# A recurrent attention with a token and channel mixer on one Trainium2 core: one batch's sum made transposed in PSUM, channel weights cut otherwise, and a new written-out order

## The chip, the core and the metric

The kernel runs on one core of one Trainium2 chip. The metric is the device time of one execution in microseconds, as the median of several runs. The profile is one execution that the hardware profiler recorded; its times count from the start of the program's span.

## What is computed

A gated linear recurrence over 768 tokens, for 4 batches and 8 heads of 48, is followed by a mixer over tokens and then over channels:

```python
for t in range(S):                                   # S = 768, D = 48, B = 4, H = 8
    state = alpha[:, :, t, :, None] * state + einsum('bhd,bhe->bhde', k[:, :, t], v[:, :, t])
    y[:, :, t] = einsum('bhd,bhde->bhe', q[:, :, t], state)
x  = y as (B, S, H * D)                              # (4, 768, 384)
h  = relu(x^T @ w_tok1) @ w_tok2                     # 768 -> 256 -> 768, over tokens
u  = x + h^T
h2 = relu(u @ w_ch1) @ w_ch2                         # 384 -> 1536 -> 384, over channels
out = u + h2
```

## The kernel before, in words

Each batch has three attention chunks of 256 tokens, numbered 0 to 11 over the four batches (chunk n belongs to batch n // 3). A chunk loads alpha, k, q and v (`ld_at`, `ld_kt`, `ld_qt`, `ld_vt`, 384 KB each), makes the decays, the masked scores and the state, and leaves two tiles `x` of 128 tokens by 384 channels. The mixer of a batch then runs, in the names of the plan:

- `t1_b_m_kc`: w_tok1 against the six x tiles, 12 matmuls of 384 columns; `ht_b_m` is the relu into bf16.
- `t2_b_i` (L883): w_tok2 against the two `ht` tiles, two matmuls for each of six token blocks; `u_b_i` (L887) is VectorE's addition of x, into the tile `u`.
- The transpose of u into `ut`. Batch 0 (`UP = (0,)`) does it on TensorE: `up_0_p` (L894), six 128 by 128 transposes for each pair of blocks, and `ut_0_p` (L746, L745), a copy of 768 columns out of PSUM. Batches 1 to 3 do it with two DMA transposes, `ux_b_half` (L729), issued from SyncE.
- `c1_b_mc_half` (L902): 12 chunks of hidden channels by two halves of the tokens, three matmuls each; `rt_b_mc_half` is the relu, on ScalarE (L873) or VectorE (L875).
- `c2_b_i_q` (L907): four groups of three matmuls for each block; `o_b_i` (L911) adds u, `st_b_i` stores 192 KB.

The weights come as fp32 loads (`ldw_`) that are cast to bf16 (`cw_`, L745 and L746): w_tok1 in two pieces, w_tok2 in two, w_ch1 in six and w_ch2 in six, 384 KB each. A piece of w_ch1 before the change is 128 rows by 768 hidden channels, so a `c1` of the chunks 0 to 5 needs the pieces 0, 1, 2 and one of the chunks 6 to 11 the pieces 3, 4, 5; in the order, chunk 11 comes first, behind the pieces 4, 3 and 5.

No scheduler runs on the device. The string `ORDER` names every operation in turn with its engine (t TensorE, s ScalarE, v VectorE, g GpSimd, y SyncE's DMA queue), and `BUFS` the buffer of every value. Each engine and each DMA queue works its own operations in that order and waits for what an operation needs. All loads and DMA transposes go through SyncE's queue, the stores through SyncE's or ScalarE's. The 19 buffers `in` hold what was loaded until it was used. Operations named `f1_` to `f12_` are fillers: matmuls over a tile of zeros (`fill`) that write a bank that nobody reads.

```python
for o in order:
    g.port_turn = o.on if o.port and o.on in ("DVE", "POOL") else None
    o.emit(o.on)
```

Of the kernel before, what the change touches and what calls it, by code (L numbers as in the profile page):

```python
# [9 lines left out]
BF16 = mybir.dt.bfloat16  # L10
# [91 lines left out]
UP = (0,)  # L102
# [18 lines left out]
def build(g):  # L121
# [8 lines left out]
    def fillers():  # L130
        for o in list(P.ops):
            nm = o.name
            if "PE" in o.eng and (nm[:4] in ("t1_0", "t2_0", "up_0") or nm.split("_")[-1][-1] in "0123" and nm[:2] not in ("t1", "t2", "up", "c1", "c2") and not nm.endswith("10") and not nm.endswith("11")):
# [182 lines left out]
    def mixer(b):  # L316
# [15 lines left out]
        us = []  # L332
        for i in range(NS):
            if i % 3 == 0:
                u = V("u")
            bank = V("one")
            o = P.op(f"t2_{b}_{i}", pe([384] * 2), m0 + (1900 + 330 * i) * sc, writes=[bank],
                     reads=[h for h, _ in hts], preds=[h for _, h in hts] + [wl[("wt2", p)] for p in range(2)],
                     emit=lambda e, i=i, bank=bank: g.tok2(bank, i, [h for h, _ in hts]))
            uo = P.op(f"u_{b}_{i}", dve(384), m0 + (1950 + 330 * i) * sc, writes=[u], reads=[bank, x[i][0]], preds=[o],  # L340
                      emit=lambda e, i=i, bank=bank, u=u: g.uadd(u, i, bank, x[i][0]))
            us.append((u, uo))
        ut = V("ut")
        uts = []
        if b in UP:
            for p in range(3):
                bank = V("one")
                o = P.op(f"up_{b}_{p}", pe([128] * 6), m0 + (3900 + 340 * p) * sc, writes=[bank],
                         reads=list(dict.fromkeys([us[2 * p][0], us[2 * p + 1][0]])),
                         preds=[us[2 * p][1], us[2 * p + 1][1]],  # L350
                         emit=lambda e, p=p, bank=bank: g.utr(bank, [us[2 * p][0], us[2 * p + 1][0]], p))
                uts.append(P.op(f"ut_{b}_{p}", either(dve(768, True), act(768)), m0 + (3950 + 340 * p) * sc, writes=[ut],
                                reads=[bank], preds=[o], emit=lambda e, p=p, bank=bank: g.utev(e, ut, bank, p)))
        else:
# [18 lines left out]
        for i in range(NS):  # L373
            hold = 4000.0 if (i >= NS - 3 and b < B - 1) else 0.0
            cuts = [(0, HD // 2), (HD // 2, HD)] if (b, i) == LAST else [(0, HD)]
            for ci, (ca, cz) in enumerate(cuts):
# [3 lines left out]
                for q4 in range(4):  # L380
                    pp = []
                    for mc in range(3 * q4, 3 * q4 + 3):
# [6 lines left out]
                          reads=[bank, us[i][0]], preds=[prev],  # L389
# [25 lines left out]
trq2t ld_at3y vs1_2g ldw_wt11y evq2v ib1t y1_1t y0_1t vs0_2g ldw_wt21y sm1_1g P3g K2t sa0_2v sm0_2g x0_1s t1_0_0_0t
f1_G0_2t G0_2t ldw_wt20y G1_2t cw_wt20g t1_0_1_0t mask0_2v x1_1s t1_0_1_1t ld_at4y ld_kt3y t1_0_1_2t lnP3s cum3t
cw_wt11s IE3s ia2t y0_2t x0_2s t1_0_0_1t t1_0_0_2t E3s t1_0_0_3t mask1_2v t1_0_1_3t ib2t y1_2t ldw_wc14y t1_0_1_4t
x1_2s t1_0_0_4t f1_t1_0_1_5t t1_0_1_5t ht_0_1v P4g cw_wt21s t1_0_0_5t ht_0_0s f3_t2_0_0t t2_0_0t t2_0_1t u_0_0v ln13s
r13s ldw_wc13y t2_0_2t u_0_1v t2_0_3t u_0_2v t2_0_5t lnP4s t2_0_4t u_0_3v u_0_5v u_0_4v up_0_0t cw_wc14s cw_wc13s
ldw_wc15y up_0_1t ld_qt3y k0a3g kk3g cum4t trk3t cw_wc15g ut_0_0v up_0_2t ut_0_2v ut_0_1s c1_0_11_0t c1_0_8_0t IE4s  # L420
c1_0_11_1t rt_0_8_0v rt_0_11_0v ldw_wc11y q0r3g qq3g c1_0_9_1t rt_0_9_1v ln14s kb3s c1_0_10_0t cw_wc11s c1_0_9_0t
rt_0_9_0v rt_0_11_1v E4s c1_0_7_0t c1_0_10_1t c1_0_7_1t ldw_wc10y r14s cw_wc10s rt_0_10_1v trq3t evk3s rt_0_7_0v
ldw_wc12y ld_vt3y cw_wc12g c1_0_2_0t c1_0_0_1t ka3g rt_0_7_1s c1_0_8_1t rt_0_10_0v vb3v vs1_3g vs0_3g rt_0_0_1v
rt_0_2_0v evq3s ld_at5y ld_qt4y c1_0_1_1t rt_0_8_1v c1_0_3_0t kc3s K3t P5g c1_0_4_1t rt_0_3_0s rt_0_1_1s q0r4g G0_3t
ld_kt4y qq4g s0_3v ln15s G1_3t sa1_3v c1_0_2_1t rt_0_2_1s mask0_3v lnP5s c1_0_1_0t c1_0_5_1t rt_0_5_1s rt_0_1_0s r15s
mask1_3v ldw_wc21y cw_wc21s k0a4g ldw_wc20y c1_0_6_1t rt_0_6_1v c1_0_4_0t kk4v ldw_wc22y c1_0_5_0t c1_0_0_0t cw_wc22s
rt_0_4_0v rt_0_0_0v cw_wc20g rt_0_4_1s c1_0_6_0t rt_0_6_0v c1_0_3_1t trq4t rt_0_3_1v cum5t trk4t ld_kt5y k0a5g
ldw_wc23y rt_0_5_0s c2_0_3_0t c2_0_5_0t evq4s kb4s evk4v ld_qt5y G1_4t mask1_4v G0_4t ld_vt4y c2_0_0_0t IE5s c2_0_0_1t
ka4g cw_wc23s c2_0_3_1t kc4s sm1_3g E5s mask0_4v ib3t y1_3t ldw_wc24y cw_wc24s c2_0_5_1t vb4g vs1_4s x1_3s ia4t
ldw_wc25y vs0_4g cw_wc25s ld_at6y y0_3t kk5v c2_0_3_2t y0_4t q0r5v trk5t evk5s qq5v K4t c2_0_0_2t sa0_4v c2_0_0_3t P6v  # L430
x0_3s ld_at7y sm0_4g o_0_0v trq5t x0_4s sa1_4v P7g evq5s lnP6s c2_0_5_2t c2_0_5_3t ld_vt5y vb5g c2_0_4_0t c2_0_4_1t
ld_kt7y kc5g G1_5t G0_5t lnP7s o_0_5v ib4t y1_4t vs1_5s mask1_5v t1_1_1_0t t1_1_1_1t sm1_4g x1_4s c2_0_4_2t c2_0_3_3t
# [61 lines left out]
class Emit:  # L494
# [386 lines left out]
    def tok2(self, bank, i, hts):  # L881
        for kc in range(NDT):
            self.pe.matmul(self.bank(bank)[:, 0:HD], lhsT=self.wt2[:, kc, i * 128 : i * 128 + 128], rhs=self.t(hts[kc]),  # L883
                           start=(kc == 0), stop=(kc == NDT - 1))
# [81 lines left out]
```

## Time and profile before

| what | value |
|---|---|
| device time, 3 runs | 162.30, 162.38, 162.38 us; median 162.38 |
| span of the profiled execution | 160.5 us |
| time of the runs outside such a span | 162.38 - 160.5 = 1.9 us |
| instructions | 3971 |
| TensorE busy | 154.6 us (96%), 1563 matmuls |
| VectorE, ScalarE, GpSimd busy | 114.9, 97.8, 80.8 us (72%, 61%, 50%) |
| DMA | 35.05 MB in 76130 packets, mean 218 GB/s |

The page gives the busy time of each engine, the span in 40 slices (a digit is the busy share in tenths), the DMA queues, and groups of instructions by line. The span leaves out what lies before the program's first and behind its last instruction; the profiled execution itself has no time of its own beside its span, so the median of the runs stands for it. In a timeline row stand the start, the time, engine, line, what is written and read, and the count.

### The profile page before, as it was taken

To read this page: it belongs to the slowest core of one execution; us is meant where nothing else is said; L and a number is where in the kernel's file an instruction comes from. 1 tells how busy PE (TensorE), PEld (TensorE's weight loads), DVE (VectorE), ACT (ScalarE), POOL (GpSimd) and SP (SyncE) were. 2 spreads that over 40 slices of the span, in tenths; PEclk is the share of its full clock that TensorE was granted. 3 is DMA by queue.
4 is the path that set the end of the run, shared out by engine and by line. 5 is a ranking of instruction groups with operands and counts; after the bars stand their busy time and mean duration, and the time that the engine had idled before them with its cause. 6 is when DMAs were issued, how large, how long until landed. Compare 5 with 4: busy or idle time off the path is not lost.

```text
span 160.5 us, 3971 instructions
## 1 busy us (share of the span) xinstructions
PE 154.6 (96%) x1563; PEld 97.1 (60%) x1563; DVE 114.9 (72%) x206; ACT 97.8 (61%) x179; POOL 80.8 (50%) x94
## 2 busy tenths in 40 slices
PE   7999989999999999999999999999999999999992
PEld 2545565766667676666667666566567665665661
DVE  6099994979889787989969758795886762464222
ACT  3789999998899955897563583269832203343000
POOL 5205897695973649389778852699523000000000
PEclk9999999999999999999999999999999999999999
DMA  4999999999999999999989999989701235111133
GB/s 122 320 324 317 317 374 311 339 333 306 316 347 324 275 278 272 210 228 319 241 202 298 239 315 204 217 196 134 196 21 62 87 79 169 49 49 53 49 129 116
DMA packets 76130, 35.05 MB, mean 218 GB/s; under 512 B 70352, under 2 KB 74320, under 8 KB 76112
## 3 DMA queue, kind: packets, MB, share of 16 engines
q1 hardware_dynamic: 73808, 31.76, 74.1%
q10 hardware_dynamic: 2304, 3.05, 5.3%
q8 instruction: 12, 0.20, 0.5%
q14 instruction: 6, 0.05, 0.1%
HBM read 25.17 MB, written 4.72 MB: 186 GB/s over the span
## 4 chain that ended last, share of the span: by engine, by line
PE 61%; DMA 12%; DVE 6%; ACT 6%; SPq 6%; POOL 4%; issue 3%; DVEq 0%; POOLq 0%
PE ps L907 22%; PE ps L902 21%; PE ps L643 11%; DMA in<-in_v_dram 6%; SPq L584 6%; DMA out_dram<-o 4%; PE ps L878 3%; PE ps L883 2%; DMA ut<-u 2%; DVE pkk L700 2%; DVE gtm L770 1%; PE ps L712 1%; DVE rt L875 1%; POOL vb L746 1%; POOL pkq L700 1%
## 5 line engine op out<-in xcount | busy, mean ns | idle before, releaser
L907 PE MATMUL ps<-wc,rt 128*128 128x384 bf16 (+1 forms) x300 | 52.4, 319 | 0.0
L902 PE MATMUL ps<-ut,wc 128*128 128x384 bf16 x288 | 50.3, 326 | 0.1
L902 PEld LDWEIGHTS <-wc 128*128 128x128 bf16 x288 | 27.1, 98 | 17.9 <-DMA ut<-u 0.6
L907 PEld LDWEIGHTS <-rt 128*128 128x128 bf16 x300 | 27.8, 98 | 16.0
L873 ACT ACTIVATE rt<-ps 128x384 bf16<-128x384 f32 x47 | 21.4, 492 | 23.6 <-PE ps L902 23.3
L875 DVE TENSOR_SCALAR rt<-ps 128x384 bf16<-128x384 f32 x49 | 25.6, 551 | 9.1 <-PE ps L902 8.9
L770 DVE TENSOR_TENSOR gtm<-ps,mk 128x1024 bf16<-128x1024 f32 x24 | 28.5, 1218 | 3.1 <-PE ps L643 2.8
L911 DVE TENSOR_TENSOR o<-ps,u 128x384 f32<-128x384 f32 (+1 forms) x25 | 13.2, 536 | 12.6 <-PE ps L907 10.1
L700 POOL TENSOR_TENSOR pkk<-in,IE 128x768 bf16<-128x768 f32 x8 | 14.5, 1817 | 3.3 <-DVE ss L844 2.3
L745 ACT CAST x<-ps 128x384 bf16<-128x384 f32 x20 | 9.2, 479 | 11.1 <-PE ps L643 9.5
L887 DVE TENSOR_TENSOR u<-ps,x 128x384 bf16<-128x384 f32 x24 | 12.0, 550 | 3.1 <-PE ps L883 2.5
L746 POOL CAST vb<-in 64x384 bf16<-64x384 f32 (+1 forms) x14 | 8.3, 594 | 10.4 <-DMA in<-in_v_dram 4.7
L692 POOL TENSOR_TENSOR in<-in,in 128x384 f32<-128x384 f32 x8 | 8.0, 1000 | 10.5 <-DVE u L887 3.8
L643 PE MATMUL ps<-rt 128*128 128x512 bf16 (+1 forms) x29 | 12.1, 515 | 1.1 <-DVE rt L541 1.1
L745 ACT CAST vb<-in 64x384 bf16<-64x384 f32 (+1 forms) x18 | 11.4, 634 | 0.8 <-DMA in<-in_v_dram 0.3
L700 POOL TENSOR_TENSOR pkq<-in,E 128x768 bf16<-128x768 f32 x6 | 10.9, 1818 | 0.6 <-DMA tpk<-pkq 0.3
L878 PE MATMUL ps<-x,wt 128*128 128x384 bf16 x48 | 11.0, 325 | 0.0
L844 POOL TENSOR_TENSOR ss<-tmp,E 128x384 bf16<-128x384 f32 x10 | 8.3, 833 | 4.2 <-DVE in L628 3.9
L841 DVE TENSOR_TENSOR tmp<-ps,ss 128x384 f32<-128x384 f32 x16 | 8.8, 552 | 1.8 <-PE ps L643 0.6
L883 PE MATMUL ps<-ht,wt 128*128 128x384 bf16 x48 | 9.1, 326 | 0.0
L643 PE MATMUL ps<-vb,gtm 128*128 128x48 bf16 x192 | 8.2, 183 | 0.2 <-DVE gtm L770 0.2
L643 PE MATMUL ps<-tpq,tpk 48*64 48x128 bf16 (+1 forms) x288 | 7.9, 218 | 0.4 <-POOL tpq L746 0.3
(94 smaller groups left out, 207.6 us busy)
## 6 DMA issues: line engine op xcount, KB each, us to landing
in<-in_alpha_dram SPq DMA_DIRECT2D x12, 384.0 KB, 5.1
in<-in_v_dram SPq DMA_DIRECT2D x12, 384.0 KB, 5.6
in<-in_k_dram SPq DMA_DIRECT2D x12, 384.0 KB, 5.2
in<-in_q_dram SPq DMA_DIRECT2D x12, 384.0 KB, 5.5
in<-in_moe_w_ch_dram SPq DMA_DIRECT2D x12, 384.0 KB, 5.9
out_dram<-o ACTq DMA_DIRECT2D x15, 192.0 KB, 1.8
in<-in_moe_w_tok_dram SPq DMA_DIRECT2D x4, 384.0 KB, 6.0
out_dram<-o SPq DMA_DIRECT2D x8, 192.0 KB, 2.2
```

The source lines that it names most:

```text
L643: return self.pe.matmul(out, lhsT=lhsT, rhs=rhs, start=start, stop=stop, skip_group_check=True)
L700: self.shared(self.eng[e].tensor_tensor(self.t(dst)[:, :, h0:h1, 0:D], self.t(src)[:, h0:h1].rearrange("p h s d -> p s h d"), bass.AP(tens ...
L745: return self.act.copy(d, s)
L770: self.nc.vector.tensor_tensor(self.t(gtm)[:, hf, :, :], self.pair(gp).rearrange("p a (j t) -> p (a j) t", t=128), bass.AP(tensor=m.tensor ...
L873: self.act.activation(d, s, AF.Relu)
L875: self.nc.vector.tensor_scalar_max(d, s, 0.0)
L878: self.pe.matmul(self.bank(bank)[:, 0:HD], lhsT=self.wt1[:, kc, m * 128 : m * 128 + 128], rhs=self.t(x), start=(kc == 0), stop=(kc == NS - 1))
L883: self.pe.matmul(self.bank(bank)[:, 0:HD], lhsT=self.wt2[:, kc, i * 128 : i * 128 + 128], rhs=self.t(hts[kc]), start=(kc == 0), stop=(kc = ...
L887: self.nc.vector.tensor_tensor(self.t(u)[:, i % 3], self.bank(bank)[:, 0:HD], self.t(x), ALU.add)
L902: self.pe.matmul(self.bank(bank)[:, 0:HD], lhsT=self.wc1[:, kc, mc * 128 : mc * 128 + 128], rhs=self.t(ut)[:, 3 * half : 3 * half + 3, kc, ...
L907: self.pe.matmul(self.bank(bank)[:, 0 : cz - ca], lhsT=self.t(rts[mc][0])[:, i * 128 : i * 128 + 128], rhs=self.wc2[:, mc, ca:cz], start=( ...
L911: self.nc.vector.tensor_tensor(self.t(o)[:, ca:cz], self.bank(bank)[:, 0 : cz - ca], self.t(u)[:, i % 3, ca:cz], ALU.add)
```

## The change

For batch 0 (`UDIR = (0,)`, `UP = ()`) u is made transposed at once. Each of six PSUM banks first gets three 128 by 128 matmuls of an x tile against the identity (`xa_0_half_j`), and then the product of the two `ht` tiles with a half of w_tok2 is added in the same bank (`tt_0_half_j`, two matmuls of 384 columns, operands swapped against `t2`). `ut_0_half_j` copies the bank (384 columns of fp32) to `ut`, on ScalarE or VectorE. VectorE's six additions `u_0_i` and the PSUM transposes are gone. The output still needs u with tokens in the partitions: two DMA transposes `un_0_half` from `ut` to `u`, on SyncE's queue, and `o_0_i` waits for them.

The w_ch1 pieces become three row blocks by 256 hidden channels, so `c1_b_mc` waits for the one piece `mc // 2`; their runs in memory are 1 KB long in place of 3 KB. The w_tok2 pieces become halves of the tokens, so a `t2` or `tt` waits for one piece. `ORDER` and `BUFS` are new from end to end. Tokens are in natural order in both kernels.

In the new order, SyncE's queue starts `ld_at0 ld_vt0 ld_kt0 ld_at2 ld_at1 ld_qt0`; the first `c1` of batch 0 waits for the 20th load (`ldw_wc14`) where it waited for the 22nd. Fillers are fewer: `f8_cumw0 f1_cumw0 f6_trk0 f1_trk0 f2_G0_1 f2_trk2 f1_trq2 f2_t1_0_1_0` stand in place of thirteen.

```diff
-UP = (0,)
+UP = ()
+UDIR = (0,)
...
+        if b in UDIR:
+            ut, us, uts = V("ut"), [], []
+            for half in range(2):
+                evs = []
+                for j in range(NM):
+                    bank = V("one")
+                    tx = x[3 * half : 3 * half + 3]
+                    xa = P.op(f"xa_{b}_{half}_{j}", pe([128] * 3), m0 + (1700 + 900 * half + 60 * j) * sc, writes=[bank],
...
+                    o = P.op(f"tt_{b}_{half}_{j}", pe([384] * 2), m0 + (1900 + 900 * half + 330 * j) * sc, writes=[bank],
+                             reads=[h for h, _ in hts], preds=[h for _, h in hts] + [xa, wl[("wt2", half)]],
...
+                    evs.append(P.op(f"ut_{b}_{half}_{j}", either(act(384), dve(384)), m0 + (1950 + 900 * half + 330 * j) * sc,
...
+                un = P.op(f"un_{b}_{half}", {"SP": (1240.0, 1240.0)}, m0 + 6000 * sc, writes=[u], reads=[ut], preds=evs,
+                          emit=lambda e, u=u, half=half: g.unat(u, ut, half), dma=("x", 1450.0, 1180.0, 480.0))
...
-                         reads=[ut], preds=(uts[0:2 + half] if b in UP else [uts[half]]) + [wl[("wc1", p)] for p in ((0, 1, 2) if mc < 6 else (3, 4, 5))],
+                         reads=[ut], preds=(uts[half] if b in UDIR else uts[0:2 + half] if b in UP else [uts[half]]) + [wl[("wc1", mc // 2)]],
...
-                          reads=[bank, us[i][0]], preds=[prev],
+                          reads=[bank, us[i][0]], preds=[prev, us[i][1]],
...
         elif nm == "wc1":
-            c, h = piece % 3, piece // 3
-            self.gated(dma(t, self.w[2][128 * c : 128 * c + 128, 768 * h : 768 * h + 768]), op)
+            w = self.w[2].rearrange("(c p) m -> p c m", p=128)
+            self.gated(dma(t.rearrange("p (c m) -> p c m", c=3), w[:, :, 256 * piece : 256 * piece + 256]), op)
...
+    def xadd(self, bank, xs, j):
+        for i, x in enumerate(xs):
+            self.mm(self.bank(bank)[:, i * 128 : i * 128 + 128], self.t(x)[:, j * 128 : j * 128 + 128], self.idn, i == 0, False)
+
+    def tok2t(self, bank, half, j, hts):
+        for kc in range(NDT):
+            self.mm(self.bank(bank)[:, 0:HD], self.t(hts[kc])[:, j * 128 : j * 128 + 128],
+                    self.wt2[:, half, kc, :], False, kc == NDT - 1)
...
+    def unat(self, u, ut, half):
+        self.nc.sync.dma_start_transpose(self.t(u).rearrange("p i (j c) -> p (i j) c", j=NM),
+                                         self.t(ut)[:, 3 * half : 3 * half + 3].rearrange("p i j t -> p (i j t)"))
```

The parts of the new order that the prediction speaks of (SyncE's queue up to the first transpose of batch 1, and TensorE around the first `c1` of batch 0 and of batch 1):

```
SyncE before: ... ldw_wc24 ldw_wc25 ld_at6 ld_at7 ld_vt5 ld_kt7 ld_at8 ld_kt6 ld_qt6 ld_qt7 ld_kt8 ld_vt6 dk6 ux_1_0
SyncE after:  ... ld_qt5 ldw_wc25 un_0_1 ld_vt5 un_0_0 ld_at6 ld_at7 ld_at8 ld_vt6 ld_qt6 ld_kt6 ld_kt7 ld_qt7 ux_1_0 ld_vt7 dk6 ux_1_1
PE after:     ... t1_0_0_5 xa_0_1_2 trq3 xa_0_1_1 tt_0_0_0 tt_0_0_2 tt_0_0_1 tt_0_1_0 tt_0_1_2 tt_0_1_1 c1_0_9_0 c1_0_8_0 trk3 c1_0_0_0
PE after:     ... t2_1_0 t2_1_5 c2_0_5_0 c2_0_5_1 c2_0_5_2 t2_1_3 t2_1_4 cum7 c2_0_5_3 c2_0_0_3 cum8 c1_1_8_0
ACT after:    ... x1_2 IE3 ht_0_1 ht_0_0 cw_wt21 ut_0_0_0 cw_wc14 ut_0_1_1
```

More of the change, by code (lines that the diff above doesn't have):

```diff
@@ L132, in fillers @@
             nm = o.name
-            if "PE" in o.eng and (nm[:4] in ("t1_0", "t2_0", "up_0") or nm.split("_")[-1][-1] in "0123" and nm[:2] not in ("t1", "t2", "up", "c1", "c2") and not nm.endswith("10") and not nm.endswith("11")):
+            if "PE" in o.eng and (nm[:4] in ("t1_0", "t2_0", "up_0", "xa_0", "tt_0") or nm.split("_")[-1][-1] in "0123" and nm[:2] not in ("t1", "t2", "up", "c1", "c2", "xa", "tt") and not nm.endswith("10") and not nm.endswith("11")):
                 bank = V("one")
@@ L331, in mixer @@
             hts.append((ht, ho))
-        us = []
-        for i in range(NS):
-            if i % 3 == 0:
-                u = V("u")
[L336 to L342, printed above, removed]
@@ L415 @@
[L415 to L419, printed above, removed]
@@ L420 @@
[L420 to L424, printed above, removed]
```

188 lines of the change are left out of this document (110 added, 78 removed), and 22 rows, old and new, of the table BUFS.

## The prediction

> **What bounds the kernel now.** I read the page first, then TensorE's waits, the windows, and the order of TensorE and of SyncE's queue around batch 0's and batch 1's first `c1`.
>
> ```profile
> span 160.5 us, 3971 instructions
> ...
> PE   7999989999999999999999999999999999999992
> ...
> DMA  4999999999999999999989999989701235111133
> ```
>
> TensorE's digits are full from the second slice to the last but one. Its waits say the same of its input:
>
> ```profile
> PE ps L643 <- DVE rt L541: 1.1, 1, 1.1
> PE ps L643 <- ACT E L683: 0.4, 1, 0.4
> PE ps L643 <- DVE gtm L770: 0.3, 2, 0.2
> PE ps L643 <- POOL tpq L746: 0.3, 1, 0.3
> ```
>
> They total 2.1 us, and none is in a mixer. But the DMA digits are full too, up to the 20th slice (80 us). The windows tell how full:
>
> ```profile
> 0.00:20.00 20.00, 18.19 (x175) 9.39 (x176) 13.99 (x39) 15.24 (x20) 8.87 (x20) 1.00 1.01 280
> 20.00:40.00 20.00, 19.50 (x206) 12.34 (x206) 16.32 (x28) 18.68 (x34) 15.62 (x18) 1.00 1.06 333
> 40.00:55.00 15.00, 14.90 (x173) 10.22 (x173) 13.14 (x19) 14.06 (x25) 9.51 (x12) 1.00 1.03 317
> 55.00:65.00 10.00, 10.00 (x116) 6.60 (x114) 7.83 (x14) 5.79 (x14) 7.37 (x8) 1.00 1.03 269
> ```
>
> The columns after the stretch are TensorE, its weight loads, VectorE, ScalarE, GpSimd (busy us), then granted clock, DMA share and GB/s. The clock is 1.00 throughout, and the DMA share is over 1.00 in each stretch to 65 us. So two resources run side by side without a hole: TensorE's order, and the transfers of SyncE's queue. A change that helps one gains only as far as the other lets it. The place where they meet is batch 1's first `c1`, behind its first DMA transpose `ux_1_0`.
>
> **TensorE's side: batch 0 starts earlier.** These are TensorE's rows of batch 0 (the second is a filler):
>
> ```profile
> 25.58 0.37 PE L643 MATMUL ps<-vb,gtm 128*128 128x48 bf16 x8
> ...
> 26.94 0.86 PE L643 MATMUL ps<-rt 128*64 128x384 f32 x2
> 27.73 2.28 PE L883 MATMUL ps<-ht,wt 128*128 128x384 bf16 x12
> 29.85 0.83 PE L894 MATMUL ps<-idn,u 128*128 128x128 bf16 x12
> ...
> 30.81 0.61 PE L712 MATMUL ps<-idn,pkk 128*128 128x128 bf16 x8
> 31.25 0.50 PE L894 MATMUL ps<-idn,u 128*128 128x128 bf16 x6
> 31.76 2.44 PE L902 MATMUL ps<-ut,wc 128*128 128x384 bf16 x14
> ```
>
> The last attention product is at 25.58, `c1` starts at 31.76. The change moves the 18 identity products (0.83 + 0.50 us of rows) ahead of the relu, where fillers stood, and drops VectorE's additions and a copy from the chain. What is late next is ScalarE, by its own queue:
>
> ```profile
> 25.99 0.48 ACT L745 CAST x<-ps 128x384 bf16<-128x384 f32 x1
> 26.37 0.83 ACT L745 CAST wt<-in 128x768 bf16<-128x768 f32 x1
> 27.10 0.49 ACT L873 ACTIVATE ht<-ps 128x384 bf16<-128x384 f32 x1
> ...
> 28.88 1.67 ACT L745 CAST wc<-in 128x768 bf16<-128x768 f32 x2
> ```
>
> In the new queue, behind the last x cast (end 25.99 + 0.48 = 26.5, which I keep: its loads, v and q of chunk 2, are the 14th and 11th where they were the 12th and 11th), come: the last `t1` (0.3), two relus (0.5 each), the cast of a w_tok2 piece (0.8), the copy `ut_0_0_0` (0.5, as a relu of the same tile), and the cast of the w_ch1 piece (1.67 / 2 = 0.8) for which `c1_0_9_0` waits. Together 26.5 + 0.3 + 1.0 + 0.8 + 0.5 + 0.8 = 29.9, with handovers some 30.2. The six `tt` banks (2.28 us from about 28.0) end at about the same time. So `c1` starts 31.76 - 30.2 = 1.5 us earlier. `trk3` and `cum4`, which stood ahead of it, now stand behind, some 0.6 us by their rows' pitch less 0.3 for `trq3`, which came forward: a lead of 1.2 us is left. Fewer fillers are worth nothing by themselves; they sat in time that TensorE waited anyway. From here to `c1_1_8_0` both orders hold the same TensorE work (151 and 148 operations, apart from the renamed ones the same set), so TensorE alone would bring batch 1's first `c1` from 67.80 to 66.6.
>
> **The queue's side: what stands ahead of `ux_1_0`.**
>
> ```profile
> 57.47 1.77 SPq L584 DMA_DIRECT2D in<-in_k_dram  x1
> 59.29 1.61 SPq L584 DMA_DIRECT2D in<-in_v_dram  x1
> 62.89 1.33 SPq L725 DMA_TRANSPOSE tpk<-pkk  x1
> 64.68 1.29 SPq L729 DMA_TRANSPOSE ut<-u  x1
> ```
>
> ```profile
> DMA  9999999999999999974269969605999979739999
> GB/s 340 331 340 325 328 331 309 377 304 306 292 277 290 301 312 317 301 218 118 60 166 297 143 117 287 127 7 133 288 294 287 198 224 382 201 84 283 293 290 359
> ...
> in<-in_k_dram SPq DMA_DIRECT2D x1, 384.0 KB, 6.5
> in<-in_v_dram SPq DMA_DIRECT2D x1, 384.0 KB, 5.8
> ...
> out_dram<-o ACTq DMA_DIRECT2D x1, 192.0 KB, 2.0
> ut<-u SPq DMA_TRANSPOSE x2, 3.0
> tpk<-pkk SPq DMA_TRANSPOSE x1, 3.4
> ```
>
> ```profile
> 62.64 1.46 PE L883 MATMUL ps<-ht,wt 128*128 128x384 bf16 x8
> ...
> 67.80 1.46 PE L902 MATMUL ps<-ut,wc 128*128 128x384 bf16 x8
> ```
>
> The first fence is SyncE's issues, the second the DMA view of 59.2 to 69.0 (40 slices of 0.245 us; then KB and us to landing), the third TensorE there. The 48th load (`ld_kt8`) lands at 57.47 + 6.5 = 64.0, the 49th at 65.1, `dk6` at 66.3, `ux_1_0` at 64.68 + 3.0 = 67.7: in order of issue. `c1_1_8_0` follows at 67.80, so TensorE's order and the queue met within 0.1 to 0.2 us. The digits show the DMA idle for parts of 63.6 to 66.3, when `dk6` and `ux_1_0` waited for their data: so the true bound of the queue before was the 48th load's landing at 64.0, and it is this that I carry over.
>
> In the changed order 48 loads, of the same kinds and sizes (16 weights, 32 of attention), stand ahead of `ux_1_0`, one fewer, and `dk6` has moved behind. Ahead of it have come both `un_0` transposes, and on ScalarE's queue three stores, with a fourth just in front, where one was. Their prices: a transpose of u is 128 x 1152 bf16, 295 KB; the GB/s row has 288, 294 and 287 in the slices in which `ux_1_0` alone ran, so 295 / 290 = 1.0 us (0.9 at the 333 GB/s of the loads; 1.4 by the distance from `dk6`'s landing to `ux_1_0`'s, which holds some waiting, so I take the value of the rate). Two make 2.0 (1.8 to 2.8). A store is 197 KB, 0.6 us at 333 GB/s; two to three more make 1.5 (1.2 to 1.8). Next, the shorter runs of w_ch1:
>
> ```profile
> in<-in_moe_w_ch_dram SPq DMA_DIRECT2D x12, 384.0 KB, 5.9
> ...
> in<-in_moe_w_tok_dram SPq DMA_DIRECT2D x4, 384.0 KB, 6.0
> ```
>
> Half of the w_tok loads already have 1 KB runs, and the four land 0.1 us later than the w_ch loads with 3 KB ones. For eight loads that bounds it at 0 to 0.8; I take 0.1, since at full queue what counts is the rate and the windows with both kinds have 280 to 333 GB/s.
>
> So the 48th load lands at 64.0 + 2.0 + 1.5 + 0.1 = 67.6, and `ux_1_0`, queued behind it, at 68.6 (67.9 to 70.8 with all ends). It can't be issued past them: all of it is one queue, worked in order. `c1_1_8_0` starts at 68.65 in place of 67.80, though TensorE could have been there at 66.6. The lead of 1.2 us is lost in a new wait of 2.0 us, and 0.85 more with it. All that TensorE has left stands behind that `c1`.
>
> [...]
>
> **After that** the remaining TensorE work is the same in both, and its pitch is a matmul's. The end:
>
> ```profile
> 147.62 9.79 PE ps L907 x72
> ...
> 157.44 0.36 DVE o L911
> ```
>
> Before, the last split block ran its 12 short matmuls at the very end; now six of them follow the last whole block, so VectorE's full addition is still under way when the last half arrives: about 0.1 us. The next meeting point, `ux_1_1`, has `ld_vt7` (1.2), `dk6` (0.9) and at most two stores between: 68.6 + 2.1 + 1.0 + up to 1.2 = 71.7 to 72.9, against nine groups of `c1` from 68.65 (27 matmuls at (1.46 - 0.33) / 7 = 0.16 us: 4.4), 73.0. That holds, barely.
>
> Sum against the profiled execution: span 160.5 + 0.85 + 0.1 = 161.45 us; with the 1.9 us by which the median of the runs exceeds the span, **163.3 us**, 0.6% slower.
>
> **The rivals.** *The lead survives (faster).* The queue isn't late: transposes and stores ride in room that the order finds, for instance because the loads' own rate differs. It decides if `ux_1_0` lands by 66.6, that is if the additions cost at least 2.0 us less than the 3.6 that I count. Then everything moves by -1.2 + 0.1, and the time is 161.3. For it: the DMA digits have holes at 63.6 to 66.3; against it: the shares over 1.00 for 65 us. *Break-even.* They cost 0.6 to 1.2 us less: `ux_1_0` lands at 67.4 to 68.0, and the time is within 0.3 of 162.4. *Worse.* The upper ends of the queue (70.8), or the next wait, on `ux_1_1`, come to bear: 164.5 and over. For it: a barely held second meeting point. A late start of batch 0 (another chain than ScalarE's) isn't a rival of the sign: up to 2 us of it vanish in the wait at `ux_1_0`.
>
> **The numbers.** The queue decides, 56% (own range 162.7 to 164.2); lead survives, 24%; break-even, 10%; worse, 10%. A measurement here tells about 0.2% (0.3 us) from no change. Faster 0.24, same 0.10, slower 0.66. The range reaches into both outer cases: 161.1 to 164.8.
>
> **What would show it.** Right: TensorE's first L902 row of batch 0 near 30.2; a wait of TensorE on DMA ut<-u of 1 to 3 us near 67, ended at about 68.6; DMA digits full to 67 us. Wrong: batch 1's first L902 row at 66 to 67 without a wait, or TensorE waits for batch 0's weights, or a later wait for a transpose.

## The result, and the profile after

The changed kernel takes 171.03 us (median of 4 runs, 170.61 to 171.6) against 162.38 us: a ratio of 1.0509, with a 95% interval of 1.046 to 1.0557. The forecast was 163.3 (161.1 to 164.8). The sign was right; of 8.6 us it had foreseen 0.9. Some executions of a kernel are over 1.5% slower than its fastest; ratios leave these out, and where a trace is of such an execution its time is given.

The page of after, with the lines that answer to those of before, and the clock that TensorE was granted:

```profile
span 169.0 us, 3955 instructions
...
PE   7987999999999979299999899959799999999992
...
PEclk9999999999999999969999999999999999999999
...
DMA  5999999999999999999999999998811109010133
```

TensorE now has holes: a 2 in the 17th slice (67.6 to 71.8 us), a 5 in the 27th, and a 6 in the clock of the 18th slice (71.8 to 76.0 us); in these places before has 9. TensorE's waits in after (us in total, times, longest):

```profile
PE ps L943 <- DMA ut<-u: 5.2, 2, 3.2
PE ps L668 <- POOL ss L869: 1.3, 1, 1.3
...
PE ps L668 <- POOL tpq L771: 1.0, 1, 1.0
...
PE ps L668 <- ACT x L770: 0.6, 1, 0.6
```

The first row is new in kind: batch 1's and batch 2's `c1` wait for their DMA transposes, 3.2 and 2.0 us. The windows of after around the first of them (columns as in the prediction):

```profile
55.00:65.00 10.00, 8.70 (x90) 5.67 (x89) 6.82 (x12) 5.38 (x12) 5.84 (x7) 1.00 1.08 300
65.00:70.00 5.00, 2.78 (x26) 1.74 (x25) 2.04 (x4) 2.99 (x7) 2.04 (x3) 1.00 1.07 255
70.00:75.00 5.00, 4.04 (x15) 2.05 (x15) 2.51 (x5) 0.22 (x1) 4.86 (x4) 0.66 1.08 206
75.00:110.00 35.00, 34.45 (x401) 21.80 (x399) 23.85 (x38) 26.22 (x50) 24.23 (x22) 1.00 1.07 240
```

From 70 to 75 us the granted clock is 0.66: TensorE lost 5.0 x 0.34 = 1.7 us there, right behind the idle time. TensorE's order in after:

```profile
27.57 2.12 PE L668 MATMUL ps<-wt,ht 128*128 128x384 bf16 x12
29.59 1.15 PE L943 MATMUL ps<-ut,wc 128*128 128x384 bf16 x6
...
67.61 0.17 PE L668 MATMUL ps<-off,idn 128*128 128x16 bf16 x1
70.96 4.28 PE L943 MATMUL ps<-ut,wc 128*128 128x384 bf16 x15 [3.17 <-DMA ut<-u]
```

Batch 0's `c1` starts at 29.59 (before 31.76), but batch 1's first `c1` only at 70.96 (before 67.80). TensorE itself was there at 67.78. SyncE's issues in after, with the time that each took:

```profile
45.45 3.52 SPq L938 DMA_TRANSPOSE u<-ut  x1
49.01 0.58 SPq L607 DMA_DIRECT2D in<-in_v_dram  x1
49.70 3.95 SPq L938 DMA_TRANSPOSE u<-ut  x1
53.69 3.15 SPq L607 DMA_DIRECT2D in<-in_alpha_dram  x3
...
65.00 3.65 SPq L754 DMA_TRANSPOSE ut<-u  x1
68.75 0.53 SPq L607 DMA_DIRECT2D in<-in_v_dram  x1
```

This is what the prediction had no row for. Both `un` transposes, and `ux_1_0` behind them, held SyncE's sequencer for 3.5 to 4.0 us, with five, four and three earlier transfers of the queue issued and not landed; in before, with two such transfers and the DMA idle for parts of 63.6 to 66.3, `ux_1_0` took 1.29. A load is often issued in about 0.5 us (`ld_vt5` above 0.58), but loads were held too: `ldw_wc23` took 3.64 us in after, and `ld_qt4` 3.01 in before, each with six transfers ahead that had not landed. `ld_at6` went out at 53.69, when `un_0_1` had landed (53.66), and landed at 58.11 (before 51.57). The DMA engines show a hole at this place; the view of 50 to 60 us, in 40 slices of 0.25 us:

```profile
DMA  9974996000089999999997779769999999999999
GB/s 235 157 84 105 266 150 3 2 8 10 9 197 317 275 312 326 329 283 290 288 291 153 157 181 184 126 129 255 318 318 327 333 366 382 350 340 315 327 324 327
```

From 51.5 to 52.75 us almost nothing moves, and from 55.25 to 56.75, behind `un_0_0`, half the rate. The first hole is no lack of issued work: the transfer ahead had landed at 51.12, and `un_0_1` and `ld_vt5`, which landed at 53.66 and 54.89, had both been issued by 49.6. So the hole lies in the transfer of `un_0_1` itself. Behind it `ld_at6` to `ld_at8` were issued late; two of them were out by 54.9, and why they moved at half the rate until 56.75 is open.

**The account.** From batch 1's first `c1` on: it starts 3.15 us later (70.96 against 67.80); half clock 1.7; the wait for `ux_2_1` 2.0; those on `tpq` 1.0 and on `x` 0.6, both behind 95 us. That is 8.45, of a span that is 8.5 us longer; before had a wait of 0.3 us of its own there, and the end adds 0.14. The 1.3 us on `ss` lie ahead of 67.6 us and went into the first wait.

Each of these waits leads back to a transfer of SyncE's queue that landed late. For `ss` and for `x` these are GpSimd and then ScalarE:

```profile
58.23 0.99 POOL L653 TENSOR_TENSOR in<-in 128x384 f32<-128x384 f32 x1 [1.90 <-DVE o L952]
59.18 0.83 POOL L869 TENSOR_TENSOR ss<-tmp,E 128x384 bf16<-128x384 f32 x1
```

```profile
94.64 1.33 ACT L770 COPY tpq<-tpk 128x1024 bf16<-128x1024 bf16 x1 [1.36 <-DMA tpk<-pkq]
95.84 1.23 ACT L770 CAST x<-ps 128x384 bf16<-128x384 f32 x3
```

The first row is `P6`, the product over alpha of chunk 6 that stands ahead of that `ss` in GpSimd's order; it starts when `ld_at6` has landed (58.11; the addition on VectorE that the row names had ended at 57.96). ScalarE's copy starts when `dq8` has landed (94.61, in before 83.00), and GpSimd's copy `tpq`, at 119.42, when `dq10` has (119.29, in before 110.05).

### The profile page after: what moved, and what is told of

Its sections match the earlier page's. It is cut to its first block, busy times and chain, and to the rows that moved or that the text cites. A ratio compares the mean times of both kernels' runs of the same rounds, so it can differ in the third digit from the quotient of the medians.

```text
span 169.0 us, 3955 instructions
## 1 busy us (share of the span) xinstructions
PE 154.3 (91%) x1553; PEld 96.8 (57%) x1553; DVE 111.7 (66%) x199; ACT 101.3 (60%) x190; POOL 78.1 (46%) x87
## 4 chain that ended last, share of the span: by engine, by line
PE 56%; DMA 18%; POOL 12%; DVE 5%; issue 4%; ACT 2%; SPq 1%; POOLq 0%; DVEq 0%
PE ps L943 18%; PE ps L948 17%; PE ps L668 13%; DMA in<-in_q_dram 9%; PE ps L903 4%; POOL pkq L725 4%; DMA ut<-u 4%; DMA tpk<-pkq 3%; POOL pkk L725 3%; PE ps L908 3%; PE ps L737 2%; DMA in<-in_alpha_dram 2%; POOL in L653 1%; DVE pkq L725 1%; DVE pkk L725 1%
## 5 line engine op out<-in xcount | busy, mean ns | idle before, releaser
L943 PE MATMUL ps<-ut,wc 128*128 128x384 bf16 x288 | 53.1, 334 | 5.2 <-DMA ut<-u 5.2
L898 ACT ACTIVATE rt<-ps 128x384 bf16<-128x384 f32 x54 | 25.2, 491 | 33.6 <-PE ps L943 33.1
L900 DVE TENSOR_SCALAR rt<-ps 128x384 bf16<-128x384 f32 x42 | 22.0, 552 | 19.1 <-PE ps L943 17.2
L770 ACT CAST vb<-in 64x384 bf16<-64x384 f32 (+1 forms) x22 | 13.5, 613 | 2.2 <-POOL vb L771 1.6
L725 POOL TENSOR_TENSOR pkq<-in,E 128x768 bf16<-128x768 f32 x7 | 12.7, 1815 | 3.1 <-PE ps L668 2.9
L653 POOL TENSOR_TENSOR in<-in 128x384 f32<-128x384 f32 x9 | 9.0, 999 | 4.4 <-DVE o L952 1.9
L912 DVE TENSOR_TENSOR u<-ps,x 128x384 bf16<-128x384 f32 x18 | 8.9, 550 | 2.4 <-PE ps L908 1.5
L668 PEld LDWEIGHTS <-tpk 48*64 48x64 bf16 (+1 forms) x288 | 6.1, 102 | 5.7 <-issue 5.1
L668 PE MATMUL ps<-rt 128*128 128x512 bf16 (+1 forms) x19 | 8.2, 547 | 1.1 <-DVE rt L564 1.1
L721 POOL TENSOR_TENSOR in<-in,lf 128x384 f32<-128x384 f32 x5 | 5.0, 998 | 8.4 <-DVE in L721 2.9
```

What stands on the lines that cost most here:

```text
L653: self.shared(self.eng[e].tensor_tensor(a[:, :, 0, :], a[:, :, 0, :], a[:, :, 1, :], ALU.mult))
L668: return self.pe.matmul(out, lhsT=lhsT, rhs=rhs, start=start, stop=stop, skip_group_check=True)
L725: self.shared(self.eng[e].tensor_tensor(self.t(dst)[:, :, h0:h1, 0:D], self.t(src)[:, h0:h1].rearrange("p h s d -> p s h d"), bass.AP(tens ...
L770: return self.act.copy(d, s)
L898: self.act.activation(d, s, AF.Relu)
L900: self.nc.vector.tensor_scalar_max(d, s, 0.0)
```

## The experiments

Ratios are to runs of before on the same chip. 1% is 1.6 us. Where operations are added or dropped, buffers are often assigned anew as well. In the expectations Theory A puts the loss on the two `un` transposes (in the runs on ScalarE's queue: on their held issue), Theory B on something else in the change (there: on the transfer itself).

### The parts of the first wait

**no_un**: after without the two `un` transposes; batch 0's output lacks u there.

```diff
-                us += [(u, un)] * 3
+                us += [None] * 3          # no un; o of batch 0 is a copy of the bank
-ORDER: ... ldw_wc25 un_0_1 ld_vt5 un_0_0 ld_at6 ...
+ORDER: ... ldw_wc25 ld_vt5 ld_at6 ...
```

> The changed kernel without the two DMA transposes un_0; the output of batch 0 is copied from PSUM, without the addition of u, which is left out. Theory A (the two transposes between the loads make the queue late): from the landing of ldw_wc25 (51.1) to that of ld_at6 (58.1) passed 7.0 us for two loads and two transposes; two loads alone are 2 x 1.2, so ux_1_0 lands 4.6 us earlier, near 66.3. TensorE is at the first c1 of batch 1 at 67.8, so its wait of 3.2 us and the stretch of half clock behind it (3.4 us, 1.7 us lost) are gone: 171.0 - 3.2 - 1.7 = 166.1 us, with the later waits (4 us) still there. Theory B (the rest of the new order makes the queue late, loads and stores): ux_1_0 lands at 69.5 or later and the time is 169 us or more.

Measured: 172.92, 168.75, 165.07 and 168.73 us, median 168.74, before 162.45. The fastest falls to Theory A's 166.1, the median lies between the theories, and the scatter is too wide for a price. The trace is of the execution of 172.92 us:

```profile
68.71 4.55 PE L940 MATMUL ps<-ut,wc 128*128 128x384 bf16 x27
74.26 1.96 PE L940 MATMUL ps<-ut,wc 128*128 128x384 bf16 x11 [1.00 <-DMA ut<-u]
```

The first wait is gone: `c1` starts at 68.71 straight behind TensorE's other work. `ux_1_0` was issued at 65.73, when its data was there, and landed at 68.67. It is gone as well in after_u_pe_swap and after_u_pe_qt10 below, which have no `un` either. So in after's order the two transposes make the first wait; the later waits stay (here 3.3 us for `ux_2_1`, with a half clock behind it; the mean clock of this execution is 0.98).

**un_together**: both transposes side by side.

```diff
-ORDER: ... un_0_1 ld_vt5 un_0_0 ld_at6 ...
+ORDER: ... un_0_1 un_0_0 ld_vt5 ld_at6 ...
```

> The changed kernel with un_0_0 issued straight behind un_0_1, ahead of ld_vt5, in place of behind it. Theory A, if what costs is the turn from loads to a transpose and back (steps of 2.5 and 2.3 us at each side, 0.9 and 1.2 between): no turn is saved, as un_0_0 and ld_vt5 only swap (2.5, 0.9, 2.3, 1.2 or so), so ux_1_0 lands within 0.5 us of 70.9 and the time within 0.5 us of 171.0. If each transpose between two loads costs its own turn: 1.2 us earlier, and with the clock some 169 to 170 us. Theory B: the same as before it, 171.0.

Measured: 170.0 us, ratio 1.0486 (1.0411 to 1.0561), as if each transpose had a turn of its own. `ux_1_0` landed at 68.94, and yet the time hardly moved: TensorE waited 2.7 us there, for it had come earlier too, and 2.3 us for `ux_2_1`.

```profile
68.98 4.33 PE L943 MATMUL ps<-ut,wc 128*128 128x384 bf16 x17 [2.72 <-DMA ut<-u]
```

TensorE was there at 66.3, and this trace has no wait on `ss`: the lead that was forecast (66.6) is there when the loads come earlier.

**fill_wait**: fillers in the wait.

```diff
-ORDER: ... cum8 c1_1_8_0 ...
+ORDER: ... cum8 f12_c1_1_8_0 f1_c1_1_8_0 c1_1_8_0 ...
```

> The changed kernel with filler matmuls (four of fp32 and one of bf16, some 2.8 us) ahead of the first c1 of batch 1, where TensorE waits 3.2 us for ux_1_0. Theory A (the half clock from 71.06 for 3.4 us follows from TensorE having stood idle): the clock stays 1.00, the matmuls behind ux_1_0 keep 0.16 us, and the time falls by 1.7 us to 169.3 us. Rival (the half clock has another cause, of load or of time): it stays and the time stays at 171.0 us.

Measured: 168.66 us, ratio 1.039 (1.0332 to 1.0448). `ux_1_0` landed late as in after (71.16), and the window shows a full clock:

```profile
70.00:75.00 5.00, 4.90 (x28) 2.53 (x27) 2.42 (x5) 1.11 (x3) 4.67 (x4) 1.00 1.10 222
```

So the half clock here (0.66 in after from 70 to 75 us, 1.00 with the fillers) is a consequence of the idle time and no cause of its own. The fillers are worth about 2 us of the 8.6 by the ratios. That all of it is the half clock is not shown: one of after's own four runs had a mean clock of 1.0 and took 170.61 us.

**pieces_alone**: before with w_ch1 in pieces of three row blocks by 256 columns.

```diff
-            self.gated(dma(t, self.w[2][128 * c : 128 * c + 128, 768 * h : 768 * h + 768]), op)
+            self.gated(dma(t.rearrange("p (c m) -> p c m", c=3), w[:, :, 256 * piece : 256 * piece + 256]), op)
```

> The kernel before, in its own order, with only the w_ch1 loads changed: three row blocks by 256 channels, 1 KB runs, and a c1 that waits for one piece. Theory A: the first c1 of batch 0 waits for ut (31.6), not for weights, so no gain; the shorter runs cost 0 to 0.1 us in each of six loads, and the time is 162.4 to 163.0 us. Theory B (the shorter runs are a main part of the late queue): ux_1_0 lands 1 us later or more, and the time is 164 us or more.

Measured: 162.8 us, ratio 1.0015 (0.9976 to 1.0053); `ux_1_0` at 67.63. The runs of 1 KB cost nothing that can be measured here (at most 0.5%).

### The price of a transpose in the queue

**before_two_tr** and **before_two_ld**: before, with two transfers of 295 KB behind `ldw_wc25` that nobody reads; once as DMA transposes, once as plain loads.

```diff
+    zz_0, zz_1: self.nc.sync.dma_start_transpose(<the other ut buffer>, <u of batch 0>)     # before_two_tr
+    zz_0, zz_1: self.nc.sync.dma_start(<the other ut buffer>, <128 x 576 fp32 of w_ch1>)    # before_two_ld
-ORDER: ... ldw_wc25 ld_at6 ...
+ORDER: ... ldw_wc25 zz_0 zz_1 ld_at6 ...
```

> before, with two DMA transposes of batch 0's u (128 x 1152 bf16 each, 295 KB) added to SyncE's queue directly behind ldw_wc25, written to the buffer ut that stands empty there and read by nobody. It measures the disputed price by itself. By the price of the prediction (1.0 each) ux_1_0 lands 2.0 us later, at 69.6, and the time is 164.4. By what the traces of after and before_un show (4.6 us for the two, with the load behind them) ux_1_0 lands at 72, TensorE waits over 3.5 us there and the clock halves: 166.5 to 169.

> before, with two plain loads of the same 295 KB each (128 rows of 2304 bytes) at the same place of the queue. By bytes alone each costs 0.9 us: ux_1_0 at 69.4, 164.2. If the price lies in transposing and not in the bytes, this kernel is 2 to 4 us faster than before_two_tr; if any transfer there costs as much (a queue that holds so many transfers at a time), the two are equal.

Measured: 165.63 us, ratio 1.0166 (1.0081 to 1.0251), with the transposes; 164.18 us, ratio 1.0056 (1.0013 to 1.0099), with the loads. With transposes the median lies between the two forecasts (164.4, and 166.5 to 169); with loads it is 1.5 us less, where 2 to 4 were expected if the price lay in transposing alone. The runs that the ratios count took 164.49 to 166.71 and 162.26 to 164.48 us. SyncE's issues of before_two_tr:

```profile
47.63 5.23 SPq L739 DMA_TRANSPOSE ut<-u  x2
52.96 1.16 SPq L589 DMA_DIRECT2D in<-in_alpha_dram  x2
54.21 1.32 SPq L589 DMA_DIRECT2D in<-in_v_dram  x1
55.64 1.09 SPq L589 DMA_DIRECT2D in<-in_k_dram  x1
```

and of before_two_ld (an execution of 165.15 us):

```profile
47.12 0.90 SPq L739 DMA_DIRECT2D ut<-in_moe_w_ch_dram  x2
48.12 2.47 SPq L589 DMA_DIRECT2D in<-in_alpha_dram  x2
50.69 3.83 SPq L589 DMA_DIRECT2D in<-in_v_dram  x1
54.63 1.03 SPq L589 DMA_DIRECT2D in<-in_k_dram  x1
```

The same bytes at the same place hold SyncE 5.23 us as transposes and 0.90 us as loads. But behind the loads the next ones are held instead: SyncE comes to `ld_kt7` 8.0 us after the first of the two transposes, and 7.5 us after the first of the two loads. So the length of an issue is not its price.

The landings give one. From the landing of `ld_vt4`, before any byte of the added transfers moved, to that of `ld_kt8`, the 48th load, it takes 15.5 us in before, 17.9 with two loads more and 18.7 with two transposes more: 1.2 and 1.6 us each. (Counted from `ldw_wc25` the loads would seem to cost 0.7, but 87% of their bytes had moved by then.) The bytes moved, from 50 to 60 us, in before_two_tr and then in before_two_ld:

```profile
GB/s 315 265 353 188 43 187 127 14 2 8 10 9 203 277 290 292 289 263 131 124 210 303 298 318 306 321 332 324 324 321 324 332 321 324 321 333 324 326 310 304
```

```profile
GB/s 270 320 316 310 344 425 320 306 330 333 310 317 333 321 326 287 178 123 83 78 71 183 178 273 327 326 300 180 149 192 289 289 293 246 241 257 290 306 324 326
```

The transposes have the hole of after again, 1.25 us from 51.75 on at 2 to 14 GB/s; the loads have a dip and no such hole.

In after, from `ldw_wc25` (51.12) to `ld_at6` (58.11), with one load between, 7.0 us pass; less two loads of 1.2 that leaves 4.6 for the two `un`, with part of a store among it. Up to the 48th load the two queues compare so (the bytes behind the last column are 284 x 13.58 = 3.86 MB in before, 265 x 18.68 = 4.95 MB in after):

```profile
50.38:63.96 13.58, 13.55 (x170) 9.32 (x169) 10.91 (x18) 10.17 (x20) 7.82 (x9) 1.00 1.04 284
```

```profile
51.12:69.80 18.68, 15.02 (x152) 9.55 (x151) 12.23 (x21) 11.36 (x23) 8.74 (x10) 1.00 1.12 265
```

At before's 284 GB/s these bytes would have taken 17.4 us. So, as an estimate, 3.8 of the 5.1 us more are the bytes of two transposes and three stores, and 1.3 are the lower rate, as long as the hole. The DMA share does not show it: it is 1.12 here, and over 1.00 in before.

**two_tr_on_act** and **after_un_on_act**: the transposes issued from ScalarE's queue, in before_two_tr and in after.

```diff
-        self.nc.sync.dma_start_transpose(
+        self.nc.scalar.dma_start_transpose(
```

> before_two_tr with the two added transposes issued from ScalarE's DMA queue in place of SyncE's, at the same place of the order. In before_two_tr their two issues held SyncE for 5.23 us (the two plain loads of the same bytes 0.90 us), and the loads behind were issued late. Theory A (the price is the held issue, in a queue full of loads): SyncE goes on issuing, at6 lands as in before_two_ld (3.4 us behind ldw_wc25, not 5.3), ux_1_0 at 70.5 or earlier; ScalarE loses about 2.6 us of issue in its place and has 39% idle time: 163.3 to 164.8. Theory B (the price is in the transfer itself, whatever queue it is on): as before_two_tr, 165.6, ux_1_0 at 71.5.

> after with both un transposes issued from ScalarE's DMA queue, nothing else changed. In after their issues held SyncE for 3.52 and 3.95 us, and ld_at6 was issued at 53.7 only. Theory A: the loads are issued on time, ux_1_0 lands at 68.5 to 69.5 in place of 70.9, the wait of 3.3 us at c1_1_8_0 shrinks to 1 to 2 us and the half clock behind it may go: 167 to 169 (the later waits stay, as in no_un, 168.7). Theory B: ux_1_0 at 70.5 or later, 170 to 171.5.

Measured: two_tr_on_act 167.01 us, ratio 1.0208 (1.0096 to 1.032). The queue did as Theory A says: `ld_at6` landed 1.1 us behind `ldw_wc25`, and the 48th load 16.1 us behind `ld_vt4` (15.5 in before), so the two transposes cost SyncE's loads 0.6 us together. The price thus goes with standing in the queue of the loads. Whether it is the held issue or the slow transfer at the head of that queue is not told apart, for both left it. The time did not follow: ScalarE was held instead, and a weight cast that TensorE needed came late. `ux_1_0` landed at 71.51, the number of Theory B, but it was issued at 68.68 only, for its data was late. ScalarE in that run, then TensorE:

```profile
50.03 2.38 ACTq L739 DMA_TRANSPOSE ut<-u  x1
...
52.44 1.41 ACTq L739 DMA_TRANSPOSE ut<-u  x1
53.88 0.83 ACT L754 CAST wc<-in 128x768 bf16<-128x768 f32 x1 [2.27 <-issue]
```

```profile
54.77 0.48 PE L916 MATMUL ps<-wc,rt 128*128 128x384 bf16 x2 [1.86 <-ACT wc L754]
```

after_un_on_act: 173.67 us, ratio 1.0611 (1.0492 to 1.073), against 1.0509 for after; the trace is of an execution of 175.09 us. ScalarE reached the two only at 51.7 and 53.1 in its own order, they landed at 58.6 and 62.1, and batch 0's output, which needs them, held its banks: TensorE waited 4.2 us for `o`. SyncE's loads waited for those landings in turn (`ld_kt6` went out at 62.15). It says nothing for or against the price on SyncE.

### What belongs to the new order

**before_u_pe** and **before_un**: before's order, with batch 0's part alone in the new form. In before_u_pe u is added to the output by 18 identity products in `c2`'s banks, in before_un by the two transposes.

```diff
-ORDER: ... t2_0_i u_0_i up_0_p ut_0_p ... c1_0_11_0 c1_0_8_0 ...
+ORDER: ... xa_0_h_j tt_0_h_j ut_0_h_j ... c1_0_8_0 c1_0_9_0 ...
+ORDER: ... ldw_wc25 un_0_0 un_0_1 ld_at6 ...                                   # before_un only
+    mm(bank, ut block, idn, start, False), three for each block of c2_0_i_0    # before_u_pe only
```

> The order of before, with only batch 0's mixer start in the new form: x added by identity products into the six banks, tt, six ut copies of 384 columns, w_ch1 pieces of 256 columns, and u added to the output by 18 identity products in c2's banks in place of the two DMA transposes. Theory A (the transposes un and the queue behind them are the main loss): nothing is added to SyncE's queue, so ux_1_0 lands at 67.6 as before; c1 of batch 0 starts 1 to 1.5 us earlier than 31.76, of which the 18 added products take 1.1, and the time is 161.6 to 162.6, equal to before. Theory B (the form of batch 0's u itself loses time, by its copies or its banks): 163.5 or more, with waits of TensorE before c1_0_8_0 or on its banks.

> The same as before_u_pe, but u of the output comes from the two DMA transposes un_0_0 and un_0_1, issued behind ldw_wc25 in the order of before. It prices the two transposes in a queue that holds what it held before. Theory A: each takes 2.5 and 0.9 us of the queue and the loads behind them are slower, so ux_1_0 lands at 71 to 73 in place of 67.6, TensorE waits 3 to 5 us ahead of c1_1_8_0, the clock halves once (1.7 us), and the time is 166.5 to 169. Theory B (a transpose costs its bytes, 1.0 each, and the re-searched order loses the rest): ux_1_0 at 69.6, time 163.5 to 164.8.

Measured: before_u_pe 164.34 us, ratio 1.0125 (1.0079 to 1.0171); before_un 165.38 us, ratio 1.0197 (1.0154 to 1.0239). before_u_pe lies in Theory B's range, though `c1` starts as early as Theory A has it; before_un lies between the two ranges. TensorE of before_u_pe:

```profile
29.80 1.14 PE L941 MATMUL ps<-ut,wc 128*128 128x384 bf16 x6
...
36.83 2.11 PE L941 MATMUL ps<-ut,wc 128*128 128x384 bf16 x12 [0.38 <-ACT tpk L768]
```

`c1` starts at 29.80 in place of 31.76. Half of this lead is order: work of chunk 4 that stood ahead of `c1` now stands behind its first six products, and the seventh starts at 31.75 against 32.73. The `c1` that begins the second row starts at 36.83, in before at 37.08, and the last `c1` of batch 0 at 44.37 against 44.43: the lead is gone before `c1` ends, about half of this second part in waits, the longest 0.4 us on ScalarE's copy. What is left on the time are the 18 products, about 0.9 us by the start of batch 1's `c1` (68.69 against 67.80), and waits behind it. The two transposes, in place of those products, cost 1.0 us more by the medians, so about 2 us in all, as an estimate.

**after_u_pe_swap**, **three_repairs**, **after_u_pe_qt10** and **four_repairs**: after, with u added by identity products (the two u_pe kernels) or with both `un` side by side and the fillers of fill_wait (the two repairs); in all of them `ux_2_1` directly behind `ux_2_0`, and in the last two `ld_qt10` ahead of `dq9` as well.

```diff
-ORDER: ... ld_kt10 dq9 dk9 ux_2_0 ld_qt10 ux_2_1 ...
+ORDER: ... ld_kt10 dq9 dk9 ux_2_0 ux_2_1 ld_qt10 ...     # after_u_pe_swap, three_repairs
+ORDER: ... ld_kt10 ld_qt10 dq9 dk9 ux_2_0 ux_2_1 ...     # after_u_pe_qt10, four_repairs
```

> after without the un transposes (u added by 18 identity products in c2's banks) and with ux_2_1 directly behind ux_2_0, ahead of ld_qt10. Theory A: both transposes and the late ux_2_1 are gone; ux_1_0 lands at 68.7 as in no_un, c1_2_0_1 no longer waits (2.2 us in after), and the time is 163.5 to 165.5. Theory B (the new order has further stalls that come up when these go): 166.5 or more.

> after with both un transposes side by side, ux_2_1 directly behind ux_2_0, and the fillers ahead of c1_1_8_0. If the parts add up (un side by side -1.0 by its run, no half clock -2.4, no wait of 2.2 at c1_2_0_1): 171.0 - 5.6 = 165.4, range 164.5 to 166.5. If the waits at ux_2_1 and behind are fed by the same late loads, moving ux_2_1 makes ld_qt10 and chunk 10 late in its place: 167.5 to 169.

> after_u_pe_swap with one more move: ld_qt10 ahead of dq9 in SyncE's queue, where it stood behind ux_2_0. In after_u_pe_swap VectorE's q0r10 waits for it until 108.0, behind it stand rt_2_1_0 and rt_2_2_0, and TensorE's c1_2_0_1 waits 2.9 us for a bank. If that is the cause, q0r10 runs before 106, the gap goes with its half clock: 163.0 to 164.5. If the queue is late there whatever comes first, ux_2_0 or ux_2_1 comes late by what ld_qt10 gains, and the time stays at 166.5 to 168.

> three_repairs with ld_qt10 ahead of dq9 as well; both un transposes are kept. If the wait at c1_2_0_1 (1.7 us in three_repairs) goes: 166.3; its distance to after_u_pe_qt10 is then the price of the two transposes in the new order (2 to 3 us). If the queue is late there whatever comes first: 167.5 to 168.5.

Measured: after_u_pe_swap 167.3 us, 1.0314 (1.0266 to 1.0362); three_repairs 167.96 us, 1.0344 (1.0296 to 1.0392); after_u_pe_qt10 166.1 us, 1.0176 (1.0096 to 1.0256); four_repairs 167.44 us, 1.024 (1.0145 to 1.0334). Moving `ux_2_1` alone did not take the later wait away: it handed it to `ld_qt10`. VectorE and then TensorE of after_u_pe_swap:

```profile
108.02 0.56 DVE L718 TENSOR_TENSOR in<-in,lf 128x384 f32<-128x384 f32 x1 [3.53 <-DMA in<-in_q_dram]
108.49 1.02 DVE L897 TENSOR_SCALAR rt<-ps 128x384 bf16<-128x384 f32 x2
```

```profile
109.10 2.40 PE L940 MATMUL ps<-ut,wc 128*128 128x384 bf16 x7 [2.73 <-DVE rt L897]
```

VectorE's `q0r10` waited 3.5 us for the load; behind it in VectorE's order stood two relus, and TensorE waited for their banks. With `ld_qt10` ahead this wait fell, and another of 1.1 us came up, for `ux_2_0`. Each move brought less than hoped; all four times are nearer to the case in which the queue is late whatever comes first.

**after_u_pe_early** and **after_early**: the last step, the transposes of batch 1 and chunk 6 ahead of the loads that stood between them; in after_u_pe_qt10, and in after with the four moves but without fillers.

```diff
-ORDER: ... ux_1_0 ld_vt7 dk6 ux_1_1 ld_kt8 k0a8 ... dq6 pq6 ...
+ORDER: ... ux_1_0 ux_1_1 dk6 dq6 ld_vt7 ld_kt8 pq6 k0a8 ...
```

> after_u_pe_qt10 with SyncE's queue changed behind ux_1_0: ux_1_1, dk6 and dq6 come ahead of ld_vt7 and ld_kt8, and on GpSimd pq6 comes ahead of k0a8 (which waits for ld_kt8). In after_u_pe_qt10 TensorE waited 1.05 us for ux_1_1 (landed 73.4) and 1.75 us ahead of G1_6, where pq6 waited for dq6 (landed 78.6, 2.6 behind the load ld_kt8). If every remaining stall of the new order is a transpose that stands behind loads, both waits go, dq6 lands by 74, and the time is 163.0 to 164.2. If the two loads then come late in their place (vb7, k0a8, chunk 7), the time stays at 165.5 to 167.

> The same moves of the queue (ux_2_1 directly behind ux_2_0, ld_qt10 ahead of dq9, ux_1_1, dk6 and dq6 ahead of ld_vt7 and ld_kt8, pq6 ahead of k0a8, both un transposes side by side), but u as in after, with both un transposes and no added fillers. What stays is the wait ahead of c1_1_8_0 (2 to 3 us) and the half clock behind it: 165 to 167. Its distance to after_u_pe_early is the price of the two transposes here, less 1.0 us of added products in the other.

Measured: 169.14 us, 1.0303 (1.0234 to 1.0371), and 170.67 us, 1.041 (1.0346 to 1.0475), both above every range that was expected. The first ratio is 0.013 higher than without the move, with intervals that just meet. In after_u_pe_qt10 GpSimd and TensorE had waited for `dq6`:

```profile
78.74 1.32 POOL L768 COPY tpq<-tpk 128x1024 bf16<-128x1024 bf16 x1 [1.62 <-DMA tpk<-pkq]
```

In after_u_pe_early `dq6` came at 74.1 in place of 78.6, and the wait stayed, now by way of `ld_vt7`, which landed at 77.66 in place of 70.68, and ScalarE's cast of it. ScalarE, then TensorE:

```profile
77.68 1.37 ACT L767 CAST vb<-in 128x768 bf16<-128x768 f32 x2 [2.17 <-DMA in<-in_v_dram]
```

```profile
79.96 0.64 PE L665 MATMUL ps<-tpq,tpk 48*64 48x128 bf16 x32 [2.05 <-POOL in L714]
```

The releaser named is GpSimd's `k0a8`, which waited for `ld_kt8` (now 78.84, 76.06 there); the relus behind ScalarE's cast end at the same time. Both stem from loads that were put back. The mechanism of the expectation's second case held, though the time came out longer still: whatever is put first, something else is late. By here the queue as a whole is behind, not one transfer in it.

**Why it is behind.** Between 40 and 107 us SyncE's queue changes between a load and a transpose 5 times in before and 16 times in after. In the trace of after a load directly behind another load lands 1.2 us after it (median of 52), a load directly behind a transpose 2.3 us (median of 10). Before has only three such loads, and they took 2.3 to 2.6 us too (`ux_1_1` at 71.06, `ld_at9` at 73.37). Seven more at 1.1 us each are 7.7 us of queue time, from a queue whose DMA share is over 1.00 from 20 to 110 us. That a transpose among loads costs more than a load there was measured for the two added ones; that these changes put the rest of the order behind was argued from the landings, and the one attempt to group them did not help.

No kernel of these beats before.

## Why the prediction was right and wrong

The forecast missed 7.6 us of the span: 2.3 at batch 1's first `c1` (70.96, forecast 68.65), and 5.2 behind it, a term that the prediction put at nothing but for 0.1 at the end.

- **"After that the remaining TensorE work is the same in both"** was the step that failed by most. The work is the same, but from that `c1` to its last matmul TensorE took 94.8 us against 89.6: 1.7 us of half clock behind the first wait, and 3.6 of waits behind 95 us, against 0.3 in before, all on transfers that landed late. The sum followed the queue to one meeting point and took it to be on time ever after. `ux_1_1` itself held, though only because TensorE was late as well. A later wait for a transpose was among the prediction's signs of being wrong. The rival "worse" had the mechanism, the upper ends of the queue and the next wait, at one chance in ten, and no price for more than one wait. The end of the kernel (0.1) was right.
- **The price of a transpose** was mis-sized: 1.0 us each, from its bytes and a rate that was read where `ux_1_0` ran alone. Among loads it was 1.6 us each (before_two_tr), where loads of the same bytes cost 1.2. The bytes were priced about rightly, by the estimate above 3.8 us for transposes and stores together against a forecast of 3.5; what was missing are the hole of 1.25 us and 0.7 us by which `ldw_wc25`, ahead of both transposes, already landed late (51.12 against 50.38). So the 48th load landed at 69.8 and not at 67.6, and `ux_1_0` at 70.9, just outside the stated ends (67.9 to 70.8). Before had the sign of it: `ld_at9` behind `ux_1_1` took 2.3 us. What makes the hole stays open.
- **"The lead of 1.2 us reaches batch 1's first `c1` at 66.6"** was wrong in after: TensorE was there at 67.8. The wait of 1.3 us for `ss` took the lead, by way of `ld_at6`, which stood behind the two `un` and landed 6.5 us later than in before. In un_together, without that wait, TensorE was there at 66.3. So the step failed because the queue was asked about at `ux_1_0` alone and not at the loads ahead of it.
- **TensorE's side up to `c1`** was right: forecast 30.2, measured 29.6, by the steps given.
- **The place of the wait** was right: TensorE waits on DMA `ut<-u` near 67, as foreseen, for 3.2 us in place of 2.0. "DMA digits full to 67 us" came true in the page's 40 slices, which are too coarse for the hole.
- **The stores** (1.5 us) were not tested apart. **The 1 KB runs** (0.1) were priced rightly: in pieces_alone the ratio is 1.0015 (0.9976 to 1.0053).

## What to carry to other kernels

A transfer is priced by what it does to the queue that it stands in: how late the loads behind it land, counted from a landing ahead of which none of its bytes moved, in rows where that queue is busy throughout. The length of its issue is not that price: here two transposes held SyncE for 5.23 us and two loads for 0.90, the loads behind the latter were held instead, and the prices were 1.6 and 1.2 us each (before_two_tr, before_two_ld). A gain of one engine is worth nothing where the next thing that it meets is fed by a queue without slack, and a queue that is late at one meeting point is to be followed to the next ones. An order is tuned as a whole: when one wait in it is mended and another of the same length comes up, the resource behind them is late, and moving single transfers did not mend that here.

## What the runs showed of the hardware

A DMA transpose of 295 KB held SyncE for 1.29 us with no earlier transfer of its queue on the way (before, issued at 129.54) and for 3.95 us with four on the way (`un_0_0` in after). Among loads its transfer had a stretch of 1.25 us at 2 to 14 GB/s (after, before_two_tr), in after with the next load already issued. The length of a wait of TensorE alone did not decide whether its clock halved. Half clock followed waits of 3.2 us (after, granted clock 0.66 from 70 to 75 us), 2.7 us (un_together, 0.75 from 66 to 71 us and 0.89 from 71 to 75) and, in two_tr_on_act, 1.9 us with one of 0.4 us behind it (0.66 from 55 to 60 us); in before_un it followed waits of 1.0 and 0.7 us, with TensorE idle for 1.7 of the 5 us from 55 to 60 (0.66 from 60 to 65). It stayed full behind 2.0 us (after, at 112: 1.00 from 110 us on), 2.3 us (un_together, at 111: the stretch from 66 to 75 us accounts for its mean clock of 0.99) and 2.1 us (after_u_pe_early, 1.00 from 75 to 85 us). Of the waits named here none over 2.3 us left the clock full, and the shorter ones did so only in part.
